# Source order instead of a scheduler's order on four engines, through 26 units of a routed expert network

## The chip, the cores and the metric

The kernel runs on one core of one Trainium2 chip. The metric is device time in microseconds (us) of one execution; the lower the better. The core has five engines that each work through a queue of their own: TensorE (PE, matmuls; its weight loads are listed apart as PEld), VectorE (DVE), ScalarE (ACT), GpSimd (POOL) and SyncE (SP, which here only issues DMAs). They wait for one another and for DMAs by semaphores.

## The reference, cut to what matters

Three layers follow one another; the second and third are the subject here. All is float32, with 1536 tokens of width 512.

```
x   = attention(q, k, v)                       # local window + block summaries, 8 heads of 64
# routed experts: 8 experts, each token goes to the one with the largest logit
idx = argmax(normalise(x) @ normalise(emb).T / tau);  gate_w = softmax probability of idx
for e in range(8):
    mask = idx == e
    h = maximum(x[mask] @ w1[e], 0.0)          # 512 -> 1024
    y[mask] = gate_w[mask] * (h @ w2[e])       # 1024 -> 512
h   = maximum(y @ w_in, 0.0)                   # dense layer: 512 -> 2048
out = (h * h) @ w_out                          # 2048 -> 512
```

With these inputs nearly all tokens of a batch of 768 go to one expert (the batch's main expert). The kernel computes the main expert for all tokens of the batch, and the few tokens of other experts in one extra block of 128 rows, which it gathers, computes and places back.

## The kernel before, in words

**Precision.** A float32 operand is split in two parts, high and low (`hl`), and a product is three matmuls instead of one: high by high, low by high, high by low. So every weight piece must be split before use: ACT copies the high part (a cast), and DVE subtracts it from the original for the low part. The same pair of steps, ACT then DVE, makes `hh` from the PSUM result `h` of the first matmul of an expert.

**Units.** The work of the PE after the attention is cut into units. A unit is one slice of 128 hidden columns for a group of 384 tokens: twelve matmuls `h` (x by w1, line 656), the ACT/DVE pair that makes `hh` (lines 687 and 688), and twelve matmuls `ya` (hh by w2, line 701). `push` writes them so that the PE runs h(n), ya(n-1), h(n+1), ya(n): while the PE is on the two pieces in between, ACT and DVE have time to make hh(n). Units 0 to 7 and 8 to 15 are the two groups of batch 0, 16 to 31 those of batch 1. At the end of a group the four accumulators `ya` in PSUM are copied out to `yt` (two by ACT, two by DVE, lines 719 to 724), and the next group reuses the same four PSUM banks. Units 32 to 95 are the dense layer, with `z` and `oa` (lines 656 and 1010) in place of h and ya.

**Side work.** Between units Python generators write further work: `tick` lets each of four queues (`means`, `rows`, `heads`, `ends`) step up to its next `yield`; `yield 6` means that six ticks pass until the next step. In this way `experts` (the normalised expert vectors, transposed by the PE into `pn`), `plan` (where the tokens of other experts go) and `first_block` with `extra` (the extra block) are woven into the PE's order. In `extra` the token numbers come from DVE masks `pt` and matmuls `pi`, POOL gathers the rows `xe` from DRAM, DVE scales them by the gate, the PE transposes them (`pxe`), ACT copies them to `xet`, and eight steps of matmuls `phe` and `pye` follow. Each step loads its own weight piece `st_x` (512 KB), and its weight half is split by ACT (`ye` high) and POOL (`ye` low).

**Weights.** All weight pieces of 512 KB (`st` of the experts, `sm` of the dense layer, `st_x`) land in one ring of four staging tiles (`stg`). A load can be issued once the tile four loads back has been read. The dense weights come as 64-bit words and are decoded by three DVE instructions (`d`, lines 896 to 903), then split by ACT and DVE (`wm`, lines 927 and 928). Twelve of the 32 pieces are decoded early and put by in DRAM (`put_by`, tile `wd`), to be read back later (`dl`).

**What sets the order.** In the attention and behind it the PE's order is that of the source (`manual_schedule(engines={ET.PE})`). On DVE, ACT, POOL and SP a scheduler of the compiler picks the order from its own model, with `high_priority` as a hint: hh is marked urgent, splits and decodes are not. What it picks is fixed when the kernel is built; on the chip each engine then runs its instructions in that order.

**PSUM slots.** The tiles tagged "m" (`pm`, `px`, `po`, `pn`, `pi`, `pxe`, `phe`, ...) share two PSUM slots in turn: a tile can be written once the tile two back has been read out.

Of the kernel before, what the change touches and what calls it, by code (L numbers as in the profile page):

```python
# [81 lines left out]
def program(ctx, tc, a):  # L82
# [157 lines left out]
    def experts():  # L240
# [11 lines left out]
        yield 6  # L252
# [241 lines left out]
    def plan():  # L494
# [19 lines left out]
        cb = xt.tile([P, 24, E], F32, tag="xt", name="cb")
# [15 lines left out]
            out=rk, in0=pr, in1=st[:, :E].unsqueeze(1).to_broadcast([P, n, E]), op=ALU.add  # L530
# [3 lines left out]
        v.tensor_scalar(out=posx, in0=posx, scalar1=-1.0, scalar2=None, op0=ALU.add)  # L534
        gf = gate.rearrange("p b j -> p (b j)")
# [104 lines left out]
    region.enter_context(tc.manual_schedule(engines={ET.PE}))  # L640
# [98 lines left out]
    def extra(i, ei, pos, new, res):  # L739
# [32 lines left out]
        v.tensor_scalar(out=xe, in0=xe, scalar1=ge[:, 2:3], scalar2=None, op0=ALU.mult)  # L772
        yield 6
# [59 lines left out]
    def first_block():  # L833
# [8 lines left out]
        s.copy(ye[:, 0], pye)  # L842
        v.tensor_tensor(out=ye[:, 1], in0=pye, in1=ye[:, 0].bitcast(F32), op=ALU.subtract)
# [64 lines left out]
    def put_by(ns):  # L908
        for n in ns:
            words[n] = dram.tile([P, DM], U32, name=f"wd{n}")  # L910
            g.dma_start(words[n], decoded(n))

    def split(ns):

        for n in ns:
# [3 lines left out]
            if n in words:  # L919
                d = dp.tile([P, DM], U32, tag="dl", name=f"dl{n}")  # L920
                nc.sync.dma_start(d, words[n])
            else:
                d = decoded(n)
# [228 lines left out]
```

## Time and profile before

| what | value |
|---|---|
| three runs | 531.96, 532.49, 532.82 us (median 532.49) |
| profiled execution | 534.48 us, of which the span of the profile is 532.5 us |
| PE busy | 504.7 us (95% of the span) |
| DVE / ACT / POOL busy | 280.9 / 196.8 / 72.6 us |
| mean granted TensorE clock | 0.988 |
| HBM traffic | 103 GB/s over the span |

All places in time are us from the start of the span. The attention takes the first 90 us or so, units 0 to 31 go up to about 253, the dense layer up to about 526, and the rest is the last store and the end of the program. In the PE's rows a group of matmuls is shown with its first start and last end; matmuls overlap, so the time that a group costs is read from one group's start to the next group's start.

### The profile page before, as it was taken

To read this page: it belongs to the slowest core of one execution; us is meant where nothing else is said; L and a number is where in the kernel's file an instruction comes from. 1 tells how busy PE (TensorE), PEld (TensorE's weight loads), DVE (VectorE), ACT (ScalarE), POOL (GpSimd) and SP (SyncE) were. 2 spreads that over 40 slices of the span, in tenths; PEclk is the share of its full clock that TensorE was granted. 3 is DMA by queue.
4 is the path that set the end of the run, shared out by engine and by line. 5 is a ranking of instruction groups with operands and counts; after the bars stand their busy time and mean duration, and the time that the engine had idled before them with its cause. 6 is when DMAs were issued, how large, how long until landed. Compare 5 with 4: busy or idle time off the path is not lost.

```text
span 532.5 us, 9937 instructions
## 1 busy us (share of the span) xinstructions
PE 504.7 (95%) x3921; PEld 458.5 (86%) x3922; DVE 280.9 (53%) x761; ACT 196.8 (37%) x454; POOL 72.6 (14%) x77
## 2 busy tenths in 40 slices
PE   6988988999997999999999999999999999999994
PEld 3777777999996988999989999999999999999993
DVE  2875879866866769599825423222232222322221
ACT  4576678314232432344636322222222222222221
POOL 1345234010012230213202000000000000000000
PEclk9898999999998999999999999999999999999999
DMA  8945647744798657254100001000010000100001
GB/s 252 266 131 173 218 158 243 248 168 160 214 340 281 200 203 237 66 178 136 42 1 20 2 0 60 0 1 0 1 59 1 1 0 2 60 1 0 1 0 65
DMA packets 18033, 55.80 MB, mean 105 GB/s; under 512 B 2151, under 2 KB 3571, under 8 KB 17982
## 3 DMA queue, kind: packets, MB, share of 16 engines
q1 hardware_dynamic: 16942, 51.71, 30.4%
q0 software_dynamic: 1040, 3.41, 1.6%
q8 instruction: 33, 0.54, 0.4%
q14 instruction: 18, 0.15, 0.1%
HBM read 45.66 MB, written 9.44 MB: 103 GB/s over the span
## 4 chain that ended last, share of the span: by engine, by line
PE 73%; DVE 10%; DMA 8%; ACT 4%; issue 2%; POOL 1%; SPq 1%; ACTq 0%; DVEq 0%; POOLq 0%
PE z L656 25%; PE oa L1010 25%; PE ya L701 7%; PE h L656 7%; DMA sm<-wm 4%; ACT sc L339 2%; DMA qk<-qk 2%; DVE d L900 1%; PE pq L318 1%; DVE d L903 1%; DVE w L287 1%; PE pa L364 1%; DMA st<-we 1%; DMA xe<-xall,idx 1%; PE pe L349 1%
## 5 line engine op out<-in xcount | busy, mean ns | idle before, releaser
L656 PE MATMUL z<-y,wm 128*128 128x384 f32 x768 | 144.2, 336 | 0.0
L1010 PE MATMUL oa<-wm,sq 128*128 128x512 f32 (+1 forms) x624 | 143.2, 376 | 0.0
L656 PEld LDWEIGHTS z<-y,wm 128*128 128x128 f32 x768 | 134.5, 188 | 3.7
L1010 PEld LDWEIGHTS oa<-wm,sq 128*128 128x128 f32 x624 | 111.6, 188 | 18.4 <-DVE sq L989 0.3
L988 DVE TENSOR_TENSOR r<-r 128x384 f32<-128x384 f32 x56 | 31.3, 558 | 155.7 <-ACT sq L984 155.7
L983 ACT ACTIVATE r<-z 128x384 f32<-128x384 f32 x64 | 31.4, 491 | 178.3 <-PE z L656 178.2
L701 PE MATMUL ya<-hh,w 128*128 128x384 f32 x384 | 74.6, 343 | 1.3 <-DVE hh L688 1.0
L656 PE MATMUL h<-x,w 128*128 128x384 f32 x384 | 73.6, 339 | 0.0
L701 PEld LDWEIGHTS ya<-hh,w 128*128 128x128 f32 x384 | 68.7, 192 | 2.4 <-DVE hh L688 1.3
L656 PEld LDWEIGHTS h<-x,w 128*128 128x128 f32 x384 | 67.0, 188 | 0.5
L989 DVE TENSOR_TENSOR sq<-r,sq 128x384 fp32r<-128x384 f32 x64 | 37.1, 580 | 12.9 <-ACT r L986 7.7
L339 ACT ACTIVATE sc<-sc,mx 128x120 f32<-128x120 f32 x96 | 30.2, 385 | 21.5 <-DVE mx L334 19.0
L984 ACT ACTIVATE sq<-r 128x384 fp32r<-128x384 f32 x64 | 33.6, 524 | 2.0
L687 ACT ACTIVATE hh<-h 128x384 fp32r<-128x384 f32 x32 | 15.7, 490 | 40.1 <-PE h L656 38.2
L876 POOL TENSOR_TENSOR y<-yt,y 128x384 fp32r<-128x384 f32 x16 | 18.4, 1152 | 68.6 <-ACT y L875 68.5
L903 DVE SCALAR_TENSOR_TENSOR d<-sm,d 128x512 uint32<-128x512 uint32 x32 | 25.1, 788 | 0.3
L896 DVE TENSOR_SCALAR d<-sm 128x512 uint32<-128x512 uint32 x32 | 16.1, 506 | 17.0 <-DMA sm<-wm 14.9
L334 DVE CUSTOM_DVE_ANT_0 sc<-pq,mask 128x120 f32<-128x120 f32 x96 | 20.8, 277 | 3.6 <-PE pq L318 3.5
L900 DVE SCALAR_TENSOR_TENSOR d<-sm,d 128x512 uint32<-128x512 uint32 x32 | 21.8, 687 | 0.4
L688 DVE SCALAR_TENSOR_TENSOR hh<-h,hh 128x384 fp32r<-128x384 f32 x32 | 17.6, 552 | 7.5 <-ACT hh L687 7.3
L286 ACT CAST w<-st 128x512 fp32r<-128x512 f32 x28 | 16.0, 624 | 15.0 <-DMA st<-we 15.0
L318 PE MATMUL pq<-qk 64*64 64x96 f32 x384 | 17.3, 263 | 4.1 <-DVE mx L334 2.0
(172 smaller groups left out, 477.6 us busy)
## 6 DMA issues: line engine op xcount, KB each, us to landing
sm<-wm SPq DMA_DIRECT2D x32, 512.0 KB, 4.5
st<-we SPq DMA_DIRECT2D x16, 512.0 KB, 4.7
qk<-qk SPq DMA_DIRECT2D x7, 768.0 KB, 9.6
vt<-vw SPq DMA_DIRECT2D x8, 648.0 KB, 7.3
st_x<-we SPq DMA_DIRECT2D x8, 512.0 KB, 4.4
xall<-xr SPq DMA_DIRECT2D x4, 768.0 KB, 5.3
wd<-d POOLq DMA_DIRECT2D x12, 256.0 KB, 5.0
dl<-wd SPq DMA_DIRECT2D x12, 256.0 KB, 2.7
```

Of the source, the lines that this page charges most:

```text
L318: t.matmul(pq[hh][o * D : (o + 1) * D, k, 96 * part : (96, KW)[part]], qk[rows, QAT + w * D : QAT + (w + 1) * D], km[rows] if part else qk ...
L334: v.tensor_tensor_reduce(out=sc[:, k], in0=pq[hh][:, k], in1=mask[:, kind], op0=ALU.add, op1=ALU.min, scale=-0.125, scalar=3e38, accum_out ...
L339: s.activation(out=sc[:, k], in_=sc[:, k], func=AF.Exp, bias=mx[:, k : k + 1], scale=-1.0)
L656: t.matmul(ps, W[:, i, c * P : (c + 1) * P], xg[:, k, c, :], start=(n == 0), stop=(n == 11))
L701: t.matmul(st["acc"][m], W[b][f][1][:, i, m * P : (m + 1) * P], hh[:, k], start=(f == 0 and i == k == 0), stop=(f == NF1 - 1 and (i, k) == ...
L900: v.scalar_tensor_tensor(out=d, in0=hw, scalar=0xC0000000, in1=d, op0=ALU.bitwise_and, op1=ALU.bitwise_or)
L903: v.scalar_tensor_tensor(out=d, in0=lw, scalar=29, in1=d, op0=ALU.logical_shift_right, op1=ALU.bitwise_or)
L983: s.activation(out=r, in_=ps, func=AF.Relu)
L984: s.activation(out=hh[:, 0], in_=r, func=AF.Square)
L988: v.tensor_tensor(out=r, in0=r, in1=r, op=ALU.mult)
L989: v.tensor_tensor(out=hh[:, 1], in0=r, in1=hh[:, 0].bitcast(F32), op=ALU.subtract)
L1010: t.matmul(st["acc"][q], hh[:, i, k * P : (k + 1) * P], WM[f][1][:, j, c0:c1], start=(f == 0 and i == j == 0), stop=(f == NF2 - 1 and (j, ...
```

## The change

The region of units 0 to 26 gets source order on all five engines; at unit 26 a new region begins, in which only the PE keeps source order, as before. For that the source is rewritten so that its order is meant: loads, splits and decodes are attached to unit numbers with `at(u, fn, ...)`, and `run(u)` writes them behind `push` of unit u, each load a unit ahead of its split or decode. Four of the twelve put-by decodes move from units up to 14 to units 23 to 25. In `extra` the gate is no longer multiplied into the gathered rows (a DVE instruction between the gather and the PE) but into the result; the first two weight pieces are requested before the transpose, and each further one two steps ahead. `plan` gets three more yields and a copy `prs` of its PSUM result; `experts` waits five ticks instead of six for its transposes.

```diff
@@ experts()
-        yield 6
+        yield 5
@@ plan()
+        prs = xt.tile([P, n, E], F32, tag="xt", name="prs")
+        v.tensor_copy(prs, pr)
...
-            out=rk, in0=pr, in1=st[:, :E].unsqueeze(1).to_broadcast([P, n, E]), op=ALU.add
+            out=rk, in0=prs, in1=st[:, :E].unsqueeze(1).to_broadcast([P, n, E]), op=ALU.add
@@ behind the attention
-    region.enter_context(tc.manual_schedule(engines={ET.PE}))
+    region.enter_context(
+        tc.manual_schedule(engines={ET.PE, ET.DVE, ET.Activation, ET.Pool, ET.SP})
+    )
@@ extra()
-        v.tensor_scalar(out=xe, in0=xe, scalar1=ge[:, 2:3], scalar2=None, op0=ALU.mult)
-        yield 6
+        yield 5
+        def load(f):
+            st = new("st", [P, 2 * DM], F32)
+            nc.sync.dma_start(st, a["we"][bass.ds(ei, 1), f].rearrange("o p n -> (o p) n"))
+            return st
+        sts = [load(0), load(1)]
+        yield
...
-                st = new("st", [P, 2 * DM], F32)
-                nc.sync.dma_start(st, a["we"][bass.ds(ei, 1), f].rearrange("o p n -> (o p) n"))
+                st = sts[f]
+                if f + 2 < NF1:
+                    sts.append(load(f + 2))
@@ first_block()
-        s.copy(ye[:, 0], pye)
-        v.tensor_tensor(out=ye[:, 1], in0=pye, in1=ye[:, 0].bitcast(F32), op=ALU.subtract)
+        gt = ex["ge"][:, 2:3]
+        s.activation(out=ye[:, 0], in_=pye, func=AF.Copy, scale=gt)
+        v.scalar_tensor_tensor(
+            out=ye[:, 1], in0=pye, scalar=gt, in1=ye[:, 0].bitcast(F32),
+            op0=ALU.mult, op1=ALU.subtract,
+        )
@@ what stands beside which unit
+    def at_weights(b, f, u):
+        at(u - 1, weight_load, b, f)
+        for o in range(2):
+            at(u, weight_split, b, f, o)
...
+    U1, U2 = 2 * NF1, 4 * NF1
...
+    for f in range(NF1):
+        at_weights(1, f, NF1 + f)
+    for n, u in zip(range(9, 2 * NF2, 2), (4, 5, 6, 7, 8, 10, 12, 14, 23, 24, 24, 25)):
+        at(u - 1, fetch, n)
+        at(u, put_by, n)
...
     for n, unit in enumerate(u1[0] + u1[1]):
         push(unit)
-        if n < 7:
-            split([n + 1])
-        elif n >= 10:
-            split([2 * n - 12, 2 * n - 11])
+        if n == 10:
+            region.close()
+            region = ExitStack()
+            region.enter_context(tc.manual_schedule(engines={ET.PE}))
+        run(U1 + n)
```

What this does to the orders, at three places. The first is the PE about halfway through the attention, at the scores `pq` of the first heads of batch 1 in tile qk_128 (`pm` and `px` are other matmuls into the shared PSUM slots, `pe` and `pa` the transposed and the weighted scores). Before, its last score matmuls and what follows:

```order
L318 MATMUL pq_857<-km_672,qk_128 64x24 x2
L318 MATMUL pq_858<-km_672,qk_128 64x24 x2
L193 MATMUL pm_899<-vt_131,ind 32x144 x12
L383 MATMUL px_914<-con,xr_182 128x128 x3
L258 MATMUL pn<-con,em 128x8 x4
L349 MATMUL pe_933<-con,sc_797 120x128 x3
L349 MATMUL pe_938<-con,sc_805 120x128 x3
```

In the changed kernel the rows ahead of the same scores are:

```order
L364 MATMUL pa_832<-vt_132,et_135 64x65 x6
L364 MATMUL pa_832<-vt_132,et_136 64x65 x6
L258 MATMUL pn<-con,em 128x8 x4
L318 MATMUL pq_867<-qk_128 64x96 x2
L318 MATMUL pq_868<-qk_128 64x96 x2
```

The four transposes `pn` have moved from behind `pm` and `px` to ahead of the scores, so `pm` is now two tiles behind an earlier `px` instead of a `po`.

The second place is ACT at units 14 to 17, where the extra block's first matmuls are near. Before:

```order
L687 ACTIVATE hh_2622<-h_2609 128x384
L286 CAST w_2606<-st_2601 128x512
L687 ACTIVATE hh_2658<-h_2645 128x384
L809 CAST ye<-st_x 128x512
L927 CAST wm_2686<-d_2682 128x512
L778 COPY xet<-pxe 128x512
L687 ACTIVATE hh_2702<-h_2689 128x384
L795 ACTIVATE he<-phe 128x128
```

And in the changed kernel:

```order
L694 ACTIVATE hh_2621<-h_2608 128x384
L286 CAST w_2640<-st_2600 128x512
L286 CAST w_2643<-st_2600 128x512
L694 ACTIVATE hh_2661<-h_2648 128x384
L792 COPY xet<-pxe 128x512
L728 COPY yt_2683<-ya_2333 128x384
L728 COPY yt_2683<-ya_2335 128x384
L810 ACTIVATE he<-phe 128x128
L824 CAST ye<-st_x 128x512
L953 CAST wm_2708<-d_2704 128x512
```

The copy `xet`, for which the extra block's first matmul waits, stood behind the cast of a weight piece (`ye`) and of a decoded one (`wm`); now it stands right behind an hh, and the two casts follow it.

The third place is DVE at units 7 to 9, around the end of the first group. Before, from the hh of unit 8 on:

```order
L688 SCALAR_TENSOR_TENSOR hh_2315<-h_2302,hh_2315 128x384
L752 TENSOR_SCALAR pt<-con,pos 128x128 x4
L719 TENSOR_TENSOR yt_2330<-ya_1862,srow_2038 128x384
L719 TENSOR_TENSOR yt_2330<-ya_1864,srow_2038 128x384
L287 TENSOR_TENSOR w_2272<-st_2270,w_2272 128x512
```

And in the changed kernel, from the end of `plan` on:

```order
L547 TENSOR_TENSOR tokg<-gr,tokg 128x12
L548 MEMSET tokg 128x12
L927 TENSOR_SCALAR d_2245<-sm_2134 128x512
L931 SCALAR_TENSOR_TENSOR d_2245<-sm_2134,d_2245 128x512
L934 SCALAR_TENSOR_TENSOR d_2245<-sm_2134,d_2245 128x512
L695 SCALAR_TENSOR_TENSOR hh_2266<-h_2253,hh_2266 128x384
L748 TENSOR_SCALAR off<-con 128x1
L751 TENSOR_SCALAR pos<-posx,off 128x12
L726 TENSOR_TENSOR yt_2296<-ya_1840,srow_2032 128x384
L726 TENSOR_TENSOR yt_2296<-ya_1842,srow_2032 128x384
```

The hh of unit 8 and the two reads of the accumulators (`yt`) now stand behind all of `plan`, its seven small writes to `tokg` and a whole decode.

## Rows read from the trace of the kernel before

**Rows 1.** The page, part 1: busy us and share of the span.
```profile
PE 504.7 (95%) x3921; PEld 458.5 (86%) x3922; DVE 280.9 (53%) x761; ACT 196.8 (37%) x454; POOL 72.6 (14%) x77
```

**Rows 2.** PE in order of time, attention: start, length, what, idle before it.
```profile
43.32 0.52 PE L383 MATMUL px<-con,xr 128*128 128x128 f32 x3 [0.16 <-PE pm L193]
45.51 0.44 PE L258 MATMUL pn<-con,em 8*128 8x8 f32 x4 [1.67 <-ACT mb L199]
...
49.34 0.40 PE L318 MATMUL pq<-qk 64*64 64x96 f32 x8
```

**Rows 3.** Stretches of 1 us: busy PE, PEld, DVE, ACT, POOL; then clock, DMA.
```profile
46.00:47.00 1.00, 1.00 (x6) 1.00 (x6) 0.74 (x3) 0.13 (x1) 0.00 (x0) 0.50 0.00 0
47.00:48.00 1.00, 1.00 (x14) 0.66 (x15) 0.00 (x0) 0.82 (x2) 0.00 (x0) 0.50 0.00 0
48.00:49.00 1.00, 1.00 (x19) 0.88 (x16) 0.04 (x1) 0.00 (x0) 0.00 (x0) 0.50 0.00 0
...
170.00:171.00 1.00, 1.00 (x5) 1.00 (x4) 0.00 (x0) 0.00 (x0) 0.00 (x0) 0.50 1.03 401
```

**Rows 4.** DVE in order of time, attention.
```profile
42.62 0.56 DVE L388 TENSOR_TENSOR x<-px,x 128x384 fp32r<-128x384 f32 x1 [0.60 <-ACT x L387]
```

**Rows 5.** Groups by line, 140 to 212 us, PE: busy, mean ns, idle before.
```profile
L701 PE MATMUL ya<-hh,w 128*128 128x384 f32 x144 | 29.3, 353 | 1.3 <-DVE hh L688 1.0 <-ACT hh L687 0.3
...
L789 PE MATMUL phe<-xet,st_x 128*128 128x128 f32 x64 | 8.8, 282 | 2.6 <-ACT xet L778 2.3 <-DVE he L796 0.2
...
L803 PE MATMUL pye<-ye,he 128*128 128x512 f32 x24 | 7.8, 428 | 1.4 <-POOL ye L810 0.9 <-ACT ye L809 0.5
...
L758 PE MATMUL pi<-tokg,pt 128*128 128x6 bf16 x12 | 1.3, 173 | 0.9 <-DVE pt L752 0.9
```

**Rows 6.** PE in order of time, the extra block's start.
```profile
167.75 1.30 PE L789 MATMUL phe<-xet,st_x 128*128 128x128 f32 x8 [2.35 <-ACT xet L778]
168.70 3.87 PE L701 MATMUL ya<-hh,w 128*128 128x384 f32 x12
```

**Rows 7.** ACT in order of time, just before that.
```profile
165.29 0.62 ACT L809 CAST ye<-st_x 128x512 fp32r<-128x512 f32 x1 [5.26 <-DMA st_x<-we]
...
167.11 0.58 ACT L778 COPY xet<-pxe 128x512 f32<-128x512 f32 x1
```

**Rows 8.** DVE in order of time, the gathered rows.
```profile
159.53 0.49 DVE L772 TENSOR_SCALAR xe<-xe,ge 128x512 f32<-128x512 f32 x1 [2.73 <-DMA xe<-xall,idx]
```

**Rows 9.** Groups by line, 140 to 212 us, the decode on DVE.
```profile
L903 DVE SCALAR_TENSOR_TENSOR d<-sm,d 128x512 uint32<-128x512 uint32 x18 | 13.9, 782 | 0.1
L900 DVE SCALAR_TENSOR_TENSOR d<-sm,d 128x512 uint32<-128x512 uint32 x18 | 12.2, 687 | 0.2
...
L896 DVE TENSOR_SCALAR d<-sm 128x512 uint32<-128x512 uint32 x17 | 8.2, 487 | 12.7 <-DMA sm<-wm 12.7
```

**Rows 10.** PE in order of time, ya(7), h(9) and ya(8).
```profile
127.46 2.27 PE L701 MATMUL ya<-hh,w 128*128 128x384 f32 x12
129.56 2.27 PE L656 MATMUL h<-x,w 128*128 128x384 f32 x12
131.67 2.24 PE L701 MATMUL ya<-hh,w 128*128 128x384 f32 x12
```

**Rows 11.** DVE in order of time: hh(7), the last row of plan, the reads.
```profile
123.20 0.56 DVE L688 SCALAR_TENSOR_TENSOR hh<-h,hh 128x384 fp32r<-128x384 f32 x1 [3.68 <-ACT hh L687]
...
127.56 0.17 DVE L534 TENSOR_SCALAR posx<-posx 128x12 f32<-128x12 f32 x1
...
129.43 1.01 DVE L719 TENSOR_TENSOR yt<-ya,srow 128x384 f32<-128x384 f32 x2
```

**Rows 12.** The page, part 6: DMA issues, KB each, us to landing.
```profile
sm<-wm SPq DMA_DIRECT2D x32, 512.0 KB, 4.5
st<-we SPq DMA_DIRECT2D x16, 512.0 KB, 4.7
```

**Rows 13.** The page, part 5: ACT's half of hh.
```profile
L687 ACT ACTIVATE hh<-h 128x384 fp32r<-128x384 f32 x32 | 15.7, 490 | 40.1 <-PE h L656 38.2
```

More of the change, by code (lines that the diff above doesn't have):

```diff
@@ L906, in decoded, with put_by @@
         return d
[L908 to L911, printed above, removed]
+    def put_by(n):
+        d = decoded(n)
+        words[n] = dram.tile([P, DM], U32, name=f"wd{n}")
+        g.dma_start(words[n], d)
     def split(ns):
@@ L918, in split @@
                 WM.append([])
[L919 to L923, printed above, removed]
-            df = d.bitcast(F32)
+            df = decoded(n).bitcast(F32)
             wp = slots[n] if n < 24 else w3p
@@ L929, in split, with at, run @@
             WM[f].append(w)
-    weights(0, range(4, NF1))
+    beside = {}
+    def at(u, fn, *args):
+        beside.setdefault(u, []).append((fn, args))
+    def run(u):
+        for fn, args in beside.pop(u, []):
+            fn(*args)
+    def at_weights(b, f, u):
[3 more added lines that the diff above has]
+    U1, U2 = 2 * NF1, 4 * NF1
+    at(-1, weight_load, 0, 4)
+    for f in range(4, NF1):
+        if f < NF1 - 1:
+            at(f - 4, weight_load, 0, f + 1)
+        for o in range(2):
+            at(f - 4, weight_split, 0, f, o)
+    for f in range(NF1):
[3 more added lines that the diff above has]
+        at(u, put_by, n)
+    for n in range(2 * NF2):
+        if n < 8:
+            u = U1 + n
+            at(u - 1, fetch, n)
+        else:
+            u = U1 + 10 + (n - 8) // 2 if n < 24 else U2 + 7 + (n - 24) // 2
+            at(u, fetch, n)
+        at(u, split, [n])
+    run(-1)
     for b in range(B):
@@ L941, in program @@
     later("rows", first_block())
-    by = list(range(9, 2 * NF2, 2))
-    def put_next():
-        if by:
-            put_by([by.pop(0)])
     for n, unit in enumerate(expert_units(0, 0)):
         push(unit)
-        if n >= 3:
-            put_next()
-    while not planned:
-        tick()
-    X2.close()
-    w1p = pool("w1p", 8, side="right")
-    weights(1, range(4))
+        if n == NF1 - 1:
+            while not planned:
+                tick()
+            X2.close()
+            w1p = pool("w1p", 8, side="right")
+        run(n)
     for n, unit in enumerate(expert_units(0, 1)):
         push(unit)
-        put_next()
-        if 2 <= n < 6:
-            weights(1, [n + 2])
+        run(NF1 + n)
     slots = [w2p] * 8 + [w1p] * 8 + [w0] * 8
-    split([0])
     u1 = [expert_units(1, gi) for gi in range(2)]
@@ L1035, in program @@
         tick()
-    for n, unit in enumerate(units[:7]):
-        push(unit)
-        if n < 2:
-            split([2 * n + 20, 2 * n + 21])
-    while queues["rows"] or queues["ends"]:
-        tick()
-    Y2.close()
-    w3p = pool("w3p", 8)
-    for n, unit in enumerate(units[7:]):
-        if n + 12 < NF2:
-            split([2 * n + 24, 2 * n + 25])
-        push(unit)
+    for n, unit in enumerate(units):
+        if n == 7:
+            while queues["rows"] or queues["ends"]:
+                tick()
+            Y2.close()
+            w3p = pool("w3p", 8)
+        push(unit)
+        run(U2 + n)
     push(None)
@@ L1060, in program @@
         yr = new_loop("yr", [P, DM], F32)
-        s.copy(yr, pye)
+        s.activation(out=yr, in_=pye, func=AF.Copy, scale=ge[:, 2:3])
         pt = psm.tile([P, NC_, P], F32, tag="m", name="pyt")
```

24 lines of the change are left out of this document (18 added, 6 removed).

## The prediction, made before the changed kernel ran

> **What bounds the kernel now.** I read the page first: PE is busy 95% of the span and no other engine is above 53% [rows 1]. So only time in which PE waits, or runs slowly, can be won. Then the PE in order of time: from 202 us to the end it has no gap, so the change can win nothing there and only lose. The gaps lie in two places: one in the middle of the attention, and a cluster between 140 and 202 us, around the extra block. For each I asked which engine ended the wait and what that engine had been doing.
>
> In the attention, PE finishes `px` and then stands 1.67 us in front of `pn`, because `pn` needs the PSUM slot of `pm`, which ACT reads late [rows 2]. Behind that wait the granted clock is 0.50, the lower of its two levels, for three microseconds and a little more, with PE busy throughout [rows 3]. The next scores `pq` start at 49.34 us.
>
> Around the extra block the waits add up as follows [rows 5]: 1.3 us in front of `ya` (hh late), 2.6 in front of `phe` (2.3 of them for ACT's `xet`), 1.4 in front of `pye` and 0.9 in front of `pi`, together 6.2 us. Behind the longest, 2.35 us, a whole `ya` takes 3.87 us [rows 6], where twelve such matmuls otherwise take 2.24 [rows 10]; the clock there is again 0.50 [rows 3]. That is another 1.6 us.
>
> Why are these late? The instructions that PE needs stand behind others that wait for a DMA. ACT had idled 5.26 us for a weight piece `st_x` before it came to `xet` at 167.11 [rows 7]. DVE had waited 2.73 us for the gathered rows, in front of the gate's multiplication [rows 8], with the next hh in its queue behind that and a decode.
>
> **The change, part by part.**
>
> *`pn` ahead of the scores.* PE no longer meets `pn` behind `pm`. What goes is the wait of 1.67 us, and the half clock: three microseconds busy at 0.50 do 1.5 us of work [rows 3], so 1.5 us. Together 3.2. What comes: `pm` now takes the slot of the `px` two back, whose last reader on DVE runs from 42.62 to 43.18 us [rows 4]. With the scores and `pn` done at about 42.6, PE waits some 0.6 us there. The four transposes cost the same at either place. Net gain 2.6 us; from below 0 (the wait merely moves to `pm` at its old length, and the clock falls as before), from above 3.2. I take 2.6, since both ends of the new wait stand in rows. Whatever of this is won at 45 us stays won if the loads of the later heads follow, and those are released by the PE's own scores, so they move with it.
>
> *No DVE instruction between gather and PE.* The multiplication with its wait of 2.73 us goes [rows 8]; the gate is now applied to the result, in two instructions that exist anyway. The hh behind it is then on time: of the 1.3 us in front of `ya`, 1.0 was DVE's.
>
> *`xet` right behind an hh, and `st_x` two steps ahead.* ACT comes to `xet` as soon as the transposes `pxe` are done, and the casts of weights stand behind it. The gathered rows were there at 159.5 us [rows 8], some 8 us ahead of the first `phe` [rows 6]; `pxe` is now half a unit later in PE's order, so it finds them. Each `st_x` has two steps of the extra block to land. Two steps hold one h and one ya, 2.1 us each by their starts [rows 10], sixteen `phe` and six `pye`, of which 64 take 8.8 us and 24 take 7.8 [rows 5], so 2.2 and 1.9: about 8 us against 4.7 for a weight piece [rows 12]. So 2.6, 1.4 and the 1.6 us of half clock go. The extra block's matmuls themselves are the same.
>
> Sum of what can be won between 140 and 202 us: 6.2 + 1.6 = 7.8 us. Of the 0.9 in front of `pi` I leave 0.4, because PE still meets the first masks just as DVE writes them. From below I take half of 7.8, if a new wait stands for every second old one.
>
> *Source order on DVE at the end of the first group.* This is what it costs. hh(7) starts on DVE at 123.20 and what follows can start at 123.7. Then come the copy `prs`, about 0.3, and `plan`, which took from 123.7 to 127.7 [rows 11]: until 128.0. Then seven writes to `tokg` of 0.2 each like the row at 127.56, until 129.4; a decode of three instructions that wait for one another, 0.49 + 0.69 + 0.78 = 2.0 us [rows 9], until 131.4; hh(8), 0.5; two small ones, 0.4. So the two reads of the accumulators, which ran at 129.43 before as one piece of 1.01 us [rows 11], are done at about 132.8 and 133.3. `ya(8)` starts at 131.67 [rows 10] and writes the same PSUM banks: its second matmul waits until 132.8 and its fourth until 133.3. That is a new wait of about 1.2 us. From below 0 (the small instructions overlap more than I assume), from above 1.2 plus a half clock as behind the wait of 1.67 us, so 1.2 + 1.6 = 2.8. I take 1.2, since it is shorter than the two waits behind which the clock fell.
>
> *Loads, splits and decodes beside the units.* The same number of each, so no work is added but the copy. An hh written behind them has room: PE needs hh(n) after ya(n-1) and h(n+1), 2 x 2.1 = 4.2 us after h(n) ends [rows 10]; ACT takes 0.49 [rows 13] and DVE 0.56 [rows 11], so about 3.1 us are spare. In units 9 to 15 DVE has per unit one hh, two low parts of a weight (0.7 each), in three of them a decode of 2.0, in two of them six masks: at most 5.2 us in a unit, with a light one behind each heavy one, on average below the 4.2 of the PE. The cover is the spare 3.1. The requests run up to four loads ahead through the ring, and a load takes 4.5 to 4.7 us [rows 12], so a request one unit earlier is just covered by the unit and the spare. Four decodes more fall to units 23 to 25: there DVE has up to 7 us in a unit, one after another, but hh(25) and hh(26) still come within their spare time by my count; I charge nothing and keep up to 2 us for the range.
>
> A rule speaks against this part. ACT's row at 165.29 shows an instruction that waits 5.26 us for its DMA, and `xet`, which needed nothing of it, comes behind it [rows 7]. The Trainium skill (Perfetto Trace Analysis, section Tensor Engine Instruction (MATMUL, LD_WEIGHTS)) says that ACT, DVE and GpSimd are strict first-in first-out queues. By that rule source order does not take such waits away, it only says who stands behind them, and where each load comes later than its split the change costs what the last rival below gives; the trace agrees, in both rows of that group.
>
> **Sum.** 2.6 + 7.8 - 0.4 - 1.2 = 8.8 us off the profiled span of 532.5. The profiled execution took 534.48 us, 0.4% over the median of the runs without a profile; I take the gain over as it is: 532.49 - 8.8 = 523.7 us.
>
> **Rivals.** Below 0.2%, about 1.1 us, a measurement of this kernel cannot tell a difference from none.
>
> *The attention gives nothing.* `pm` or the scores take over the wait of `pn`. For it: two slots only, and DVE and ACT are both in the middle of their softmax work there. Against it: the reader that `pm` waits for is done at 43.18 [rows 4]. Time: 532.49 - 6.2 = 526.3.
>
> *The new queue order costs its own gaps.* The wait at `ya(8)` brings the half clock with it (2.8 instead of 1.2), and units 23 to 26 cost 2 us. Time: 523.7 + 1.6 + 2 = 527.3.
>
> *No difference.* The waits around the extra block come back in other places, because what is late is the ring of four staging tiles, not the order: 7.8 + 0.4 back and nothing from the attention. For it: 12.7 us of DVE idling for decoded weights [rows 9]. Against it: those waits are on DVE, and PE stood still for other things. Time: about 532.
>
> *Slower.* In units 8 to 15 each weight load comes only when its split's turn has come, and the hh stands behind the split. One mechanism: SP's queue is held by a read-back `dl` or by the number of the extra block's expert, so the load goes out late. A load that is requested only at its split costs 4.7 us, 1.6 over the spare 3.1; over eight units 12.8 us, so 523.7 + 12.8 = 536.5. It decides from 1.1 us over the spare in each of eight units, waits of 4.2 us. Against it: by my count of when tiles come free, SP has the loads out two to three microseconds before they are needed.
>
> **How the numbers follow.** The forecast has 0.60, nothing from the attention 0.13, new gaps 0.14, no difference 0.06, slower 0.07. The forecast's own range is 521 (3.2 from the attention, nothing new at `ya(8)`, `pi` free) to 526. The whole range reaches from 520.5, that end with half a microsecond of other small waits, to 529, which takes in the two rivals that win less; above it lie the last two. Faster by more than 0.2%: 0.60 + 0.13 + 0.14 and a small part of the no-difference case, 0.88; same 0.05; slower 0.07.
>
> **What the changed profile would show.** `pn` without a wait, `pm` or `px` with some 0.6 us, no half clock in the middle of the attention, and the first h about 2.6 us earlier. A wait of `ya` for DVE `yt` of about 1 us in unit 8. No wait in front of `phe`, `pye` and `xet`, and no clock below 1.00 after 100 us. From about unit 23 no PE gap. The prediction is wrong if ACT or DVE show idle time for `st` or `sm` in front of an hh and PE waits for that hh, or if the clock falls behind the wait at `ya(8)`.

## The result, and the profile after

The changed kernel takes 524.59 us (median of 4 runs, 522.59 to 526.44), the kernel before 532.23 (530.98 to 532.82) beside it: ratio 0.9866, 95% interval 0.9835 to 0.9896, 7.6 us less. In the three later comparisons the median of before lay at 531.65, 531.37 and 532.01. The profiled execution after took 523.62 us with a span of 521.8. Ratios are of runs in the chip's fast state; only B1 below has slow ones, two of its 12, which its median holds and its ratio does not.

The page of after, part 1: busy us, share of the span and instructions of each engine.

```profile
PE 501.8 (96%) x3922; PEld 456.4 (87%) x3922; DVE 285.8 (55%) x761; ACT 195.4 (37%) x454; POOL 74.5 (14%) x77
```

Against [rows 1], DVE's sum is 4.9 us larger and PE's 2.9 us smaller. Where the PE's time went is in its own rows. PE of after in order of time, at the five places that the argument needs (line 663 is h and z, 708 ya, 804 phe, 1065 oa):

```profile
39.30 0.41 PE L258 MATMUL pn<-con,em 8*128 8x8 f32 x4
...
40.61 0.94 PE L193 MATMUL pm<-vt,ind 96*32 96x144 f32 x24
41.57 0.55 PE L383 MATMUL px<-con,xr 128*128 128x128 f32 x3
...
44.21 0.40 PE L318 MATMUL pq<-qk 64*64 64x96 f32 x8
...
50.72 0.52 PE L383 MATMUL px<-con,xr 128*128 128x128 f32 x3 [0.93 <-DVE x L388]
...
127.12 2.80 PE L708 MATMUL ya<-hh,w 128*128 128x384 f32 x12
129.76 2.25 PE L663 MATMUL h<-x,w 128*128 128x384 f32 x12
...
160.25 1.05 PE L804 MATMUL phe<-xet,st_x 128*128 128x128 f32 x8
...
221.61 0.97 PE L708 MATMUL ya<-hh,w 128*128 128x384 f32 x4 [0.61 <-DVE hh L695]
...
248.57 2.70 PE L1065 MATMUL oa<-wm,sq 128*128 128x512 f32 x9 [0.97 <-ACT yt L728]
```

What answers to [rows 2]: `pn` has no wait, and the scores `pq` that answer to those at 49.34 come at 44.21. What answers to [rows 6]: the first `phe` has no wait. New are a `ya(8)` of 2.64 us up to the next h (2.10 from `ya(7)` to its next h in [rows 10]), a wait of 0.61 us inside `ya(26)` and one of 0.97 us in the first `oa`. DVE of after at these places:

```profile
40.32 0.18 DVE L260 TENSOR_TENSOR en_hl<-pn,en_hl 128x32 fp32r<-128x32 f32 x1
40.96 0.56 DVE L388 TENSOR_TENSOR x<-px,x 128x384 fp32r<-128x384 f32 x1 [0.46 <-ACT x L387]
...
123.45 0.17 DVE L538 TENSOR_SCALAR posx<-posx 128x12 f32<-128x12 f32 x1
...
124.45 0.41 DVE L927 TENSOR_SCALAR d<-sm 128x512 uint32<-128x512 uint32 x1
...
126.23 0.55 DVE L695 SCALAR_TENSOR_TENSOR hh<-h,hh 128x384 fp32r<-128x384 f32 x1
...
127.02 1.01 DVE L726 TENSOR_TENSOR yt<-ya,srow 128x384 f32<-128x384 f32 x2
...
212.24 1.39 DVE L934 SCALAR_TENSOR_TENSOR d<-sm,d 128x512 uint32<-128x512 uint32 x1
...
218.15 1.14 DVE L927 TENSOR_SCALAR d<-sm 128x512 uint32<-128x512 uint32 x1 [1.00 <-DMA wd<-d]
...
221.01 0.55 DVE L695 SCALAR_TENSOR_TENSOR hh<-h,hh 128x384 fp32r<-128x384 f32 x1
```

Read it from the bottom: the hh for which `ya(26)` waits stands behind decodes, and one of those waited 1.00 us for its tile `d` to be written out to DRAM. At 127.02 the two reads `yt` come just as `ya(8)` wants their banks; between the last row of `plan` and them stand the writes to `tokg`, a decode and hh(8). Before, they began 2.24 us ahead of `ya(8)` ([rows 10, 11]). ACT of after, the copy `xet` and, in the scheduler's region, what stands ahead of the last group's reads `yt`:

```profile
157.90 0.49 ACT L694 ACTIVATE hh<-h 128x384 fp32r<-128x384 f32 x1 [2.71 <-PE h L663]
158.33 0.59 ACT L792 COPY xet<-pxe 128x512 f32<-128x512 f32 x1
...
244.46 0.62 ACT L953 CAST wm<-d 128x512 fp32r<-128x512 f32 x1 [4.48 <-DVE d L934]
...
248.06 0.84 ACT L728 COPY yt<-ya 128x384 f32<-128x384 f32 x2
```

`xet` follows its hh at once, where it stood behind 5.26 us of waiting in [rows 7]. Groups by line from h(10) to h(21) of after, PE (busy, mean ns, idle before), as [rows 5]:

```profile
L708 PE MATMUL ya<-hh,w 128*128 128x384 f32 x133 | 25.5, 338 | 0.0
...
L804 PE MATMUL phe<-xet,st_x 128*128 128x128 f32 x64 | 8.5, 276 | 0.0
L818 PE MATMUL pye<-ye,he 128*128 128x512 f32 x24 | 7.6, 422 | 0.0
L765 PE MATMUL pi<-tokg,pt 128*128 128x6 bf16 x12 | 1.0, 171 | 0.0
```

All 6.2 us of waits are gone there. Windows of after (busy PE, PEld, DVE, ACT, POOL; clock, DMA):

```profile
44.00:45.00 1.00, 1.00 (x43) 0.79 (x42) 0.76 (x3) 0.97 (x4) 0.00 (x0) 1.00 0.05 7
160.00:170.00 10.00, 9.96 (x64) 9.39 (x63) 7.54 (x14) 4.15 (x10) 3.05 (x3) 1.00 0.41 129
...
230.00:240.00 10.00, 10.00 (x61) 9.84 (x60) 10.00 (x17) 6.16 (x13) 5.87 (x4) 1.00 0.64 199
240.00:250.00 10.00, 9.03 (x49) 8.19 (x48) 10.00 (x19) 5.28 (x11) 1.02 (x1) 1.00 0.64 214
```

The clock is 1.00 where it was 0.50 in [rows 3], and DVE has become full (busy 10.00 of 10 us) from 230 us on.

The next table cuts every profiled execution at the same starts on the PE: up to the first h, to h(10), to h(21), to z(0), to z(3), in us; then the PE waits between h(10) and h(21), added up over the extra block's lines and `ya`. The letters are those of the experiments below. The last column does not hold the half clock: between h(10) and h(21) the clock is at 0.50 for some 3.4 us, which costs 1.7, in before, A1 and B2, and in no other row.

| kernel | h(0) | to h(10) | to h(21) | to z(0) | to z(3) | waits |
|---|---|---|---|---|---|---|
| before | 83.11 | 50.64 | 69.83 | 49.62 | 13.87 | 6.2 |
| after | 78.56 | 51.20 | 60.44 | 50.63 | 15.49 | 0 |
| A1 pn alone | 79.51 | 50.65 | 68.32 | 49.60 | 13.88 | 4.9 |
| A2 pn back | 80.80 | 51.23 | 60.46 | 50.63 | 15.48 | 0 |
| B1 scheduler | 79.06 | 50.65 | 66.01 | 57.62 | 13.87 | 4.7 |
| B2 scheduler, early put-bys | 79.22 | 50.65 | 70.67 | 49.80 | 13.86 | 7.7 |
| B3 DVE to the scheduler | 78.50 | 50.66 | 62.15 | 53.43 | 15.35 | 1.3 |
| C1 extra block alone | 81.19 | 50.65 | 66.48 | 49.59 | 13.88 | 4.7 |
| C2 gate back | 79.70 | 51.23 | 61.45 | 50.63 | 15.54 | 1.0 |
| C3 requests back | 79.07 | 51.24 | 62.08 | 50.64 | 15.41 | 1.2 |
| D1 more tiles d | 79.56 | 51.24 | 60.42 | 50.47 | 15.05 | 0 |
| D2 no decode at 7 | 78.34 | 50.65 | 61.92 | 50.61 | 15.43 | 1.0 |
| D3 later end | 79.18 | 51.22 | 60.42 | 52.57 | 21.48 | 0 |
| D4 spread put-bys | 78.81 | 51.22 | 63.64 | 51.21 | 15.55 | 3.0 |

After against before: -4.55, +0.56, -9.39, +1.01, +1.62, together -10.75 us. That is more than the 7.6 us of the medians, because the profiled execution of before took 534.48 us, 2 to 3 over its medians, and the profiled one of after 1 less than its own. Of the -4.55, 1.67 us were there before the first moved row (`pq` of the preceding group at 38.01 and 36.34); ten of the fourteen profiles show the clock at 0.50 for 3 to 10 us between 10 and 22 us (before and after among them), two between 29 and 33 us (B2, D3), two not before 50 us (B3, C2), so the first column carries differences that the change did not make.

### The profile page after: what moved, and what is told of

Same layout as the page of the kernel before. It is cut to its first block, busy times and chain, and to the rows that moved or that the text cites. A ratio compares the mean times of both kernels' runs of the same rounds, so it can differ in the third digit from the quotient of the medians.

```text
span 521.8 us, 9927 instructions
## 1 busy us (share of the span) xinstructions
PE 501.8 (96%) x3922; PEld 456.4 (87%) x3922; DVE 285.8 (55%) x761; ACT 195.4 (37%) x454; POOL 74.5 (14%) x77
## 4 chain that ended last, share of the span: by engine, by line
PE 77%; DVE 9%; ACT 5%; DMA 4%; issue 2%; POOL 1%; SPq 0%; ACTq 0%; POOLq 0%
PE oa L1065 25%; PE z L663 25%; PE h L663 9%; PE ya L708 9%; ACT sc L339 3%; DMA vt<-vw 2%; DMA wd<-d 2%; PE phe L804 1%; DVE wm L954 1%; PE pq L318 1%; PE pye L818 1%; PE pl L434 1%; DVE d L931 1%; DVE d L934 1%; DVE sc L334 1%
## 5 line engine op out<-in xcount | busy, mean ns | idle before, releaser
L708 PEld LDWEIGHTS ya<-hh,w 128*128 128x128 f32 x384 | 67.2, 188 | 2.0 <-DVE hh L695 0.9
L934 DVE SCALAR_TENSOR_TENSOR d<-sm,d 128x512 uint32<-128x512 uint32 x32 | 27.2, 854 | 0.7
L953 ACT CAST wm<-d 128x512 fp32r<-128x512 f32 x20 | 12.4, 620 | 40.1 <-DVE d L934 38.4
L895 POOL TENSOR_TENSOR y<-yt,y 128x384 fp32r<-128x384 f32 x16 | 20.2, 1270 | 46.5 <-ACT y L894 46.5
L931 DVE SCALAR_TENSOR_TENSOR d<-sm,d 128x512 uint32<-128x512 uint32 x32 | 24.0, 755 | 0.6
L287 DVE TENSOR_TENSOR w<-st,w 128x512 fp32r<-128x512 f32 x28 | 20.0, 752 | 3.2 <-ACT w L286 2.9
L942 POOL DMA_DIRECT2D wd<-d x12 | 6.8, 567 | 85.5 <-DVE d L934 56.2
```

Of the source, the lines that this page charges most:

```text
L708: t.matmul(st["acc"][m], W[b][f][1][:, i, m * P : (m + 1) * P], hh[:, k], start=(f == 0 and i == k == 0), stop=(f == NF1 - 1 and (i, k) == ...
L895: g.tensor_tensor(out=y[:, 1, m], in0=yf, in1=y[:, 0, m].bitcast(F32), op=ALU.subtract)
L931: v.scalar_tensor_tensor(out=d, in0=hw, scalar=0xC0000000, in1=d, op0=ALU.bitwise_and, op1=ALU.bitwise_or)
L934: v.scalar_tensor_tensor(out=d, in0=lw, scalar=29, in1=d, op0=ALU.logical_shift_right, op1=ALU.bitwise_or)
```

## The experiments

### A. The place of pn

A1 is the kernel before with one line changed:

```diff
@@ experts()
-        yield 6
+        yield 5
```

> The kernel before with only the transposes pn moved ahead of the scores. Theory (the place of pn is worth what the two traces show between the scores pq at 38 and those behind pn): 3.0 to 3.5 us faster than before, ratio 0.993 to 0.994, no wait of pn and no half clock between 40 and 50 us. Rival (the attention ran faster in the changed kernel only because its start differed, or the time is lost again behind the attention): within 1.0 us of before, ratio 0.998 to 1.002.

Measured: 529.03 us (12 runs) against 531.65, ratio 0.9957 (0.9936 to 0.9979): 2.6 us less, below what was expected, with 3.0 us still inside the interval. From the `pq` ahead of the place to the second one behind it A1 takes 10.82 us (37.33 to 48.15), before 14.28 (38.01 to 52.29), so 3.46 are won. Then a part is given back at the next `px`, PE of A1:

```profile
51.69 0.52 PE L383 MATMUL px<-con,xr 128*128 128x128 f32 x3 [1.63 <-DVE x L388]
```

There before waits 1.06 us. Up to this `px` the difference is 17.26 - 14.36 = 2.90 us.

A2 is the changed kernel with the same line put back.

> The changed kernel with only the transposes pn moved back behind pm and px. Theory: 3.0 to 3.5 us slower than the changed kernel, ratio to before 0.992 to 0.993, with a wait of pn of 1.5 us or more and the clock at 0.50 behind it. Rival (the place of pn is worth nothing): like the changed kernel, ratio 0.986 to 0.987.

Measured: 525.92 us (6 runs), ratio 0.9901 (0.9868 to 0.9935) against 0.9866 of the changed kernel, 1.9 us by the two ratios, whose intervals overlap. PE of A2, and a window behind it:

```profile
43.75 0.41 PE L258 MATMUL pn<-con,em 8*128 8x8 f32 x4 [1.67 <-ACT mb L199]
```

```profile
46.00:47.00 1.00, 1.00 (x14) 0.44 (x14) 0.55 (x2) 0.00 (x0) 0.00 (x0) 0.50 0.00 0
```

The wait of 1.67 us and the half clock behind it are back as in [rows 2, 3]. Up to the later `px` it takes 16.61 us against 14.38: 2.2. The 3.0 to 3.5 us were not reached, and A2's time alone cannot be told from the changed kernel's; by these rows and by A1's time the rival, that the place is worth nothing, falls.

### B. The order of the queues

B1 is the changed kernel, with its whole rewritten source, but the scheduler's order on four engines:

```diff
-        tc.manual_schedule(engines={ET.PE, ET.DVE, ET.Activation, ET.Pool, ET.SP})
+        tc.manual_schedule(engines={ET.PE})
```

> The changed kernel with its whole rewritten source, but with the scheduler's order on DVE, ACT, POOL and SP in units 0 to 26 too. Theory (the queue order is what wins, since it says who stands behind a wait for a DMA): 4 us or more slower than the changed kernel, ratio to before 0.994 or higher, with PE waits in front of phe, ya or pye that end with ACT or DVE. Rival (the extra block's early requests and the gate at the result win, and the scheduler orders the rewritten source as well): within 1.5 us of the changed kernel, ratio 0.984 to 0.989.

Measured: 535.76 us (12 runs), ratio 1.0047 (1.0013 to 1.0082): slower than before, 9.6 us behind the changed kernel by the ratios. Two things add up. The waits around the extra block are there, 4.7 us, and from h(10) to h(21) the same source takes 5.6 us more than in source order (66.01 against 60.44); and from h(21) to z(0) it takes 57.62 us against 50.63. DVE of B1 there, PE, and a window behind its waits:

```profile
211.09 0.43 DVE L927 TENSOR_SCALAR d<-sm 128x512 uint32<-128x512 uint32 x1 [2.04 <-DMA wd<-d]
...
216.61 0.43 DVE L927 TENSOR_SCALAR d<-sm 128x512 uint32<-128x512 uint32 x1 [1.64 <-DMA wd<-d]
...
217.56 0.55 DVE L893 TENSOR_TENSOR yt<-yt,pd 128x384 f32<-128x384 f32 x1
```

```profile
218.16 0.61 PE L888 MATMUL pd<-pm,ye 128*128 128x384 f32 x2 [2.07 <-DVE yt L893]
...
221.10 3.71 PE L708 MATMUL ya<-hh,w 128*128 128x384 f32 x10 [1.20 <-DVE yt L726]
```

```profile
222.00:224.00 2.00, 2.00 (x8) 2.00 (x8) 2.00 (x3) 1.41 (x3) 1.18 (x1) 0.50 0.02 5
```

The scheduler put decodes that wait for a tile still being written to DRAM ahead of the `yt` for which PE waits. These waits and a shorter one are 3.6 us; behind them the clock is at 0.50 from 221 to 227 us, which costs about as much again. So in B1 the four late put-by decodes are mixed into the comparison. B2 takes them out: B1 with the twelve put-bys at units 3 to 14, as before.

```diff
-    for n, u in zip(range(9, 2 * NF2, 2), (4, 5, 6, 7, 8, 10, 12, 14, 23, 24, 24, 25)):
+    for n, u in zip(range(9, 2 * NF2, 2), range(3, 15)):
```

> The rewritten source with the scheduler's order on DVE, ACT, POOL and SP, as in the run before of that name, but with the twelve put-by decodes at units 3 to 14 as in the kernel before, none at 23 to 25. Theory (the four late decodes cost that run 5 us in the scheduler's order, between 216 and 228 us, and the waits around the extra block the rest): 4 to 6 us faster than that run, ratio to before 0.994 to 0.997, so still 4 us or more behind the changed kernel. Rival (only the late decodes were wrong, the scheduler orders the rest as well as the source): 0.986 to 0.989. Other rival (the late decodes are harmless): 1.003 or higher, like that run.

Measured: 532.72 us (12 runs), ratio 1.0001 (0.9979 to 1.0023): 2.5 us better than B1 by the ratios (the intervals just overlap), less than the theory's 4 to 6, and 7.2 us behind the changed kernel. From h(21) to z(0) it loses nothing (49.80). Between h(10) and h(21), where DVE now runs 35 instructions of decodes instead of B1's 28, it is 4.7 us longer than B1: it waits 7.7 us, and the half clock is back. ACT of B2 at its longest wait, and the decode on DVE for which the cast waits:

```profile
157.92 0.62 ACT L824 CAST ye<-st_x 128x512 fp32r<-128x512 f32 x1 [3.28 <-DMA st_x<-we]
...
164.27 0.62 ACT L953 CAST wm<-d 128x512 fp32r<-128x512 f32 x1 [5.34 <-DVE d L934]
...
165.17 0.58 ACT L792 COPY xet<-pxe 128x512 f32<-128x512 f32 x1
```

```profile
162.36 0.43 DVE L927 TENSOR_SCALAR d<-sm 128x512 uint32<-128x512 uint32 x1 [2.84 <-DMA sm<-wm]
```

Behind this `xet` PE waits 3.61 us in front of `phe`. It is the picture of [rows 7], with a cast of a decoded piece in the place of `ye`: what PE needs needs nothing of the DMA, and stands behind something that does. The Trainium skill (Perfetto Trace Analysis, section Tensor Engine Instruction (MATMUL, LD_WEIGHTS)) calls ACT, DVE and GpSimd strict first-in first-out queues; the three rows of ACT agree.

B3 leaves DVE alone to the scheduler:

```diff
-        tc.manual_schedule(engines={ET.PE, ET.DVE, ET.Activation, ET.Pool, ET.SP})
+        tc.manual_schedule(engines={ET.PE, ET.Activation, ET.Pool, ET.SP})
```

> The changed kernel with DVE alone in the scheduler's order in units 0 to 26, ACT, POOL and SP in source order. Theory (it is the order on both ACT and DVE that wins; with the rewritten source and the scheduler on all four the time was 535.8, with the source order 524.6): 3 to 7 us slower than the changed kernel, ratio to before 0.992 to 1.000, with waits that end with DVE in front of phe or pd. Rival (ACT's xet behind the wait for st_x was the whole loss): within 1.5 us of the changed kernel, 0.986 to 0.989. Other rival (DVE's order is the whole loss): like the run with the scheduler on all four, 1.003 or higher.

Measured: 527.15 us (6 runs), ratio 0.9915 (0.9892 to 0.9939), 2.6 us behind the changed kernel, a little better than expected. Source order on ACT, POOL and SP together brings 7 us against B1 (1.0047 to 0.9915). By the columns 3.9 of it lie between h(10) and h(21), where no `phe` waits, 4.2 between h(21) and z(0), and 1.5 are lost again up to z(3). What is left is DVE's: 1.3 us in front of `pye`, most of it for `he`, and again a put-by, behind whose wait the clock is at 0.50 from 207 to 210 us. DVE of B3, and PE:

```profile
203.37 0.43 DVE L927 TENSOR_SCALAR d<-sm 128x512 uint32<-128x512 uint32 x1 [3.92 <-DMA wd<-d]
...
204.85 0.55 DVE L695 SCALAR_TENSOR_TENSOR hh<-h,hh 128x384 fp32r<-128x384 f32 x1
```

```profile
205.45 0.96 PE L708 MATMUL ya<-hh,w 128*128 128x384 f32 x4 [1.84 <-DVE hh L695]
```

### C. The extra block's own part

C1 is the kernel before with the two hunks of the change in `extra()` (requests two steps ahead, `yield 5`, load, `yield`, and no multiplication of `xe`) and the one in `first_block()` (the gate at the result), in the scheduler's order.

> The kernel before with only the extra block's part: weight pieces st_x requested two steps ahead and the gate at the result, all in the scheduler's order. Theory (both belong to the gain of units 10 to 21, but the queue order has to come with them): 2 to 5 us faster than before, ratio 0.990 to 0.996. Rival (this part alone is the gain around the extra block): 8 to 9.5 us faster, ratio 0.982 to 0.985. Other rival (it is nothing without the queue order): within 1 us of before.

Measured: 531.39 us (12 runs), ratio 1.0003 (0.9979 to 1.0026): nothing. The wait in front of `phe` changed its cause and not its length, PE of C1:

```profile
166.47 1.16 PE L797 MATMUL phe<-xet,st_x 128*128 128x128 f32 x8 [2.37 <-DVE he L804]
```

`xet` is on time now, but ACT's `he` stands behind a cast `wm` that waited 3.63 us for a decode. Then C2 and C3 take one half each out of the changed kernel.

```diff
@@ C2, extra(), and first_block() as before
+        v.tensor_scalar(out=xe, in0=xe, scalar1=ge[:, 2:3], scalar2=None, op0=ALU.mult)
         yield 5
@@ C3, extra(), with yield 6 and no sts
-                st = sts[f]
-                if f + 2 < NF1:
-                    sts.append(load(f + 2))
+                st = new("st", [P, 2 * DM], F32)
+                nc.sync.dma_start(st, a["we"][bass.ds(ei, 1), f].rearrange("o p n -> (o p) n"))
```

> The changed kernel with the gate multiplied into the gathered rows again, so a DVE instruction between the gather and the transposes pxe, in source order; the weight pieces stay two steps ahead. Theory (the multiplication costs what it makes late: the hh behind it, as the 1.0 us in front of ya before): 0.5 to 1.5 us slower than the changed kernel, ratio to before 0.988 to 0.990, with a DVE wait for xe and a PE wait of ya for hh behind it. Rival (where it stands now the gathered rows are there in time): ratio 0.986 to 0.988 and no such wait.

> The changed kernel with each st_x requested in its own step again. Theory (two steps of 8 us cover a load of 4.7 us, one of 3.7 us does not): waits of phe for st_x of about 1 us in most of the eight steps, 3 us or more slower than the changed kernel, ratio to before 0.992 or higher. Rival (SP works ahead of the other engines, so the request goes out as soon as a staging tile is free, wherever it is written): within 1 us of the changed kernel, ratio 0.986 to 0.989, no wait of phe.

Measured: C2 524.86 us (5 runs), ratio 0.9860 (0.9834 to 0.9885); C3 525.59 us (6 runs), 0.9881 (0.9858 to 0.9904). Neither can be told from the changed kernel by time; from h(10) to h(21) they take 1.0 and 1.6 us more in the profiles. So the rivals hold by time, and their reasons in part: in C2 the gathered rows are not there in time, DVE waits 5.01 us for them, but between h(10) and h(21) no `ya` waits for DVE, and one `phe` waits 1.0 for `he`; in C3 two of the eight `phe` wait, 0.5 and 0.7 us. Both halves taken back together were not tried. Groups by line of C3, h(10) to h(21):

```profile
L795 PE MATMUL phe<-xet,st_x 128*128 128x128 f32 x64 | 8.7, 278 | 1.2 <-DVE d L925 0.7 <-DMA st_x<-we 0.5
```

### D. The new gaps, and attempts to close them

```diff
@@ D1, decoded() and fetch()
-        d = dp.tile([P, DM], U32, tag="d", name=f"d{n}")
+        d = dp.tile([P, DM], U32, tag="d", name=f"d{n}", bufs=4)
-            st = staged[n] = dp.tile([P, DM], U32, tag="dl", name=f"dl{n}")
+            st = staged[n] = dp.tile([P, DM], U32, tag="dl", name=f"dl{n}", bufs=2)
@@ D2, units of the put-bys
-(4, 5, 6, 7, 8, 10, 12, 14, 23, 24, 24, 25)
+(4, 5, 6, 8, 9, 10, 12, 14, 23, 24, 24, 25)
@@ D3: region.close() and the new region not at unit 26 (n == 10), but at the dense layer's n == 7
@@ D4, units of the put-bys
+(4, 5, 6, 7, 8, 10, 12, 14, 16, 18, 20, 22)
```

> The changed kernel with four instead of three tiles for decoded words (d), and two instead of three for those read back (dl), which pays for the room. Theory (at unit 26 a decode waits 1.00 us for a tile whose put-by has not landed, and hh stands behind it): the wait of the decode and the one of ya(26), 0.61 us, are gone; 0.5 to 1.0 us faster than the changed kernel, ratio to before 0.984 to 0.986. Rival (DVE is full from there on, so the next wait takes it back): ya(26) without a wait, but the wait at oa(0) grows by as much, and the ratio stays at 0.986 to 0.988.

Measured: 524.86 us (4 runs), 0.9869 (0.9841 to 0.9897). The decode's wait of 1.00 us is gone, but `ya(26)` still waits 0.45 us: DVE works without a gap up to that hh. At the first `oa` 0.57 is left of 0.97, and a later `oa` (265.88) waits 1.00 for `sq`. The theory, that the tile was the cause, falls; the rival holds: DVE is full. The total does not price the fourth tile alone, since D1 also has one tile fewer for the words read back: up to z(3) its columns are 0.6 us shorter than the changed kernel's, and behind z(3) it takes 1.8 us more.

> The changed kernel with the put-by decodes of units 7 and 8 one unit later (8 and 9), so that no decode stands between plan and the reads of the accumulators yt. Theory (the decode of 1.9 us on DVE is what makes ya(8) 0.55 us longer): from ya(8) to h(10) 2.1 us instead of 2.64, about 0.5 us faster, which is below what the ratio can tell (0.985 to 0.987). Rival (ya(8) is slowed by something else, or the decodes then hold hh(9) or hh(10)): 2.6 us there still, or a new wait of as much in units 9 to 11.

Measured: 524.65 us (6 runs), 0.9883 (0.9853 to 0.9913). `ya(8)` to h(10) takes 2.08 us (126.91 to 128.99), so the decode was what cost 0.56. But the decode ahead of the masks now waits 0.82 us for its words, so the masks are late, PE of D2:

```profile
138.51 0.57 PE L765 MATMUL pi<-tokg,pt 128*128 128x6 bf16 x3 [1.03 <-DVE pt L759]
```

So theory and rival are both right, one after the other, and h(10) to h(21) is 1.5 us longer.

> The changed kernel with the source order on all engines up to unit 39 instead of 26. Theory (in the scheduler's order four casts and a decode were put ahead of the reads yt, for which the first oa waited 0.97 us, at a cost of about 1.6): that wait is gone, 1 to 2 us faster than the changed kernel, ratio 0.982 to 0.985. Rival (DVE is full between 230 and 260 us, so in source order every hh and sq stands behind two splits and a decode): waits of ya and oa for hh and sq there, 2 us or more slower, ratio 0.990 or higher.

Measured: 533.15 us (12 runs), 1.0031 (1.0014 to 1.0048), 8.8 us behind the changed kernel; the rival by far. DVE of D3, in source order around the last group's end:

```profile
254.77 0.42 DVE L927 TENSOR_SCALAR d<-sm 128x512 uint32<-128x512 uint32 x1
...
257.33 0.69 DVE L954 TENSOR_TENSOR wm<-d,wm 128x512 fp32r<-128x512 f32 x1 [0.69 <-ACT wm L953]
...
259.35 0.56 DVE L1039 TENSOR_TENSOR sq<-r,sq 128x384 fp32r<-128x384 f32 x1 [0.72 <-ACT r L1036]
259.83 1.01 DVE L893 TENSOR_TENSOR yt<-yt,pd 128x384 f32<-128x384 f32 x2
```

A decode and two low parts stand as one block ahead of `sq` and `yt`, and DVE idles between them for ACT: from 240 and from 250 us on it is busy only 8.65 and 7.38 of 10 us. PE waits 2.60 us for that `yt`, and 1.28 (`yt` of DVE), 0.93 (hh of ACT) and 1.46 us (`yt` of ACT) ahead of it.

> The changed kernel with its last four put-by decodes at units 16, 18, 20 and 22 instead of 23, 24, 24 and 25. Theory (DVE is busy 9 of 10 between 210 and 220 us and 6 to 7 of 10 between 170 and 190, so the decodes fit there): no wait of ya(26), 0.6 to 1.5 us faster than the changed kernel, ratio to before 0.983 to 0.986. Rival (four more loads through the ring of staging tiles delay the extra block's st_x, or DVE's he): waits of phe for he or st_x between 160 and 195 us, 1 us or more slower, ratio 0.988 or higher.

Measured: 528.79 us (12 runs), 0.9941 (0.9919 to 0.9962), 4.0 us behind the changed kernel. `ya(26)` has no wait any more, as the theory says, but between h(10) and h(21) 3.0 us of waits appear, PE of D4:

```profile
169.18 1.16 PE L804 MATMUL phe<-xet,st_x 128*128 128x128 f32 x8 [1.82 <-DVE he L811]
...
181.71 1.13 PE L804 MATMUL phe<-xet,st_x 128*128 128x128 f32 x8 [1.16 <-DMA st_x<-we]
```

Both halves of the rival show: one wait for DVE, one for the weight piece. The wait in front of the first `oa` is there too, 1.39 us for DVE's `yt`; DVE is full from 210 to 250 us. No version tried was faster than the changed kernel beyond what the runs can tell.

## Why the prediction was right, and where it was not

The forecast was 523.7 us, its case "all terms"; measured were 524.59. The total came out, several of its steps did not, and that it came so close is in part luck: 2.6 us lost behind h(21), which the forecast put at nothing, stand against about 1.4 us that two other terms gave beyond it.

**`pn`.** Predicted 2.6 us net: 3.2 won, 0.6 for a new wait of `pm`. A1 shows 3.46 won, 0.57 lost, 2.90 net in the trace and 2.6 in the medians. The size is right, the step on the new wait is wrong, and with it the account of the slots as strictly the tile two back. "`pm` now takes the slot of the `px` two back" does not hold: `pm` starts at 40.61, behind the end of `en_hl` (40.50), which reads `pn`, and ahead of the end of `x` (41.52), which reads that `px`. It was `px` that started behind `x`, without a wait. So the rows fit only with `pm` in `pn`'s slot. In A1 the loss came ten microseconds later, at a `px` that waits for DVE's `x`. That wait is between 0.73 and 1.64 us in the profiles with `pn` ahead, 1.06 in before, and in two of them (B1, C2) the half clock follows it: the half clock is not gone from the attention for good.

**140 to 202 us.** Predicted 7.8 less 0.4. From h(10) to h(21) the traces give 9.4 against before, and 7.9 against A1, which has the order of before there: executions of one order differ by 1.5 us, so no single trace gives this term closer. All 6.2 us of waits and the 1.7 of half clock went, the 0.4 at `pi` too. But two mechanisms named there are not what did it. The requests two steps ahead and the gate at the result gave nothing alone (C1), and next to nothing was lost when either was taken back (C2, C3). With the scheduler's order the rewritten source is no faster than before (B2), although it holds what `pn` wins. What wins there is who stands behind a wait for a DMA: with the same source the scheduler's order takes 5.6 us more from h(10) to h(21) (B1), of which the order on ACT, POOL and SP gives back 3.9 (B3) and DVE's the last 1.7. ACT was not set apart from POOL and SP; the rows show `xet` on ACT. But the late put-bys belong to the gain, which the prediction did not say: in the scheduler's order the stretch is 4.7 us longer with all of them early (B2 against B1), in source order 3.2 longer with the last four at units 16 to 22 (D4). Source order with all of them at units 3 to 14 was not tried.

**`ya(8)`.** Predicted 1.2 us, measured 0.56. The cause is the one named, the decode (D2). The size was off because the seven writes to `tokg` overlap (1.0 us from 123.53 to 124.5, not 1.4) and the copy, the decode and the small rows came out shorter, `plan` itself 0.3 longer, so that the reads `yt` were done 0.4 and 0.9 us after `ya(8)` began, not 1.1 and 1.6.

**Units 23 and up.** "I charge nothing", and from unit 23 on no PE gap: wrong. PE loses 1.0 us up to z(0) and 1.6 up to z(3). The step that failed is the count of spare time unit by unit; it left out what is not done earlier. On DVE between h(10) and h(21) before ran 43 of the three-instruction decodes' instructions, after only 26; from h(26) to z(3) it is 22 before and 34 after. These 12 instructions take about 8 us of an engine that is busy 10.00 of 10 us there. B2, with early put-bys and the scheduler, has 22 and neither gap. D1 shows that one tile more does not help, D4 that earlier units have no room that costs nothing. A count tells where the pile comes from. By h(26) before had run 71 of the 96 decode instructions, after 54, and in both sources 60 stand ahead of unit 26: before's scheduler had pulled 11 of the later ones forward, which source order up to unit 26 rules out, and after is 6 behind. The late put-bys alone are not the cause of the gap at `oa`: D4, without them, has run 64 by h(26), and still has it. No run with source order keeps those 11 early, so what that would be worth stays open.

**The slower rival**, loads that go out late behind SP, did not show: between h(10) and h(21) no `st` makes PE wait, and ACT idled only 0.8 us for `st` between 130 and 205 us. The range and the other rivals are not tested by a total that fell where the forecast had put it.

**The base.** The terms came to 8.8 us; the medians show 7.6. In sum, with the last term as what is left over: 2.6 for `pn` (predicted 2.6), -0.56 (-1.2), 2.6 lost behind h(21) (0), which leaves about 8.2 for units 10 to 21 (7.4).

## What to carry over

Where an engine waits for a DMA, look at what stands behind it in its queue and who needs that: moving the waiting instruction behind the needed one was worth more here than starting the DMA earlier. A fixed order paid here while the engines had spare time: carried on into the stretch where DVE had been busy 10.00 of 10 us, the same rule on all engines cost 8.8 us, and DVE then idled for ACT (D3). If work is moved later, count it per stretch on the engine that does it, before and after, and not only unit by unit.

## What was not expected of the hardware

The clock does not go by the length of the PE's wait alone. Behind 2.35 us (before, [rows 6]) and behind 1.67 us (before and A2) it fell to 0.50, the lower of its two levels; behind 2.37 us in C1 and 1.63 us in A1 it stayed at 1.00. At the `px` of A1's row C2 waited as long, and there it fell. PE of C2 and the window behind it, then the window behind A1's wait:

```profile
50.64 0.88 PE L383 MATMUL px<-con,xr 128*128 128x128 f32 x3 [1.64 <-DVE x L388]
```

```profile
51.00:52.00 1.00, 1.00 (x7) 1.00 (x6) 0.71 (x8) 1.00 (x5) 0.92 (x2) 0.50 0.49 154
```

```profile
52.00:53.00 1.00, 1.00 (x14) 0.83 (x14) 0.76 (x8) 1.00 (x5) 0.92 (x2) 1.00 1.06 369
```

So a gain or a loss by the half clock behind one wait is not to be counted on from one profile.

The third instruction of a decode took 0.69 us as a rule and 1.39 us at 212.24 in after, while POOL ran its subtraction `y` from 211.76 to 213.08. The Trainium skill (SBUF — State Buffer, section Who interferes with whom) says that a DVE instruction with two inputs in SBUF contends with a GpSimd instruction that reads SBUF; this pair of rows agrees. A first instruction, which has one input, took 1.14 us instead of 0.41 at 218.15 beside another such `y` as well; that sentence does not cover it. Over the whole trace the second and third instructions of all decodes took 51.2 us after and 46.9 before, 4.3 of the 4.9 us by which DVE's sum rose, and each one of them that took over 1 us, in either trace, ran beside a tensor_tensor of POOL. So DVE was fuller than a count of durations from quiet rows gives.
